# One chained run for the output matmuls of a half unit, in place of two pieces

## The chip, the cores and the metric

The kernel runs on one core of a Trainium2 chip. The metric is the device time of one execution in microseconds (us). TensorE is PE in the profile (PEld is its weight load), VectorE is DVE, ScalarE is ACT, GpSimd is POOL, and SyncE, which issues most DMAs, is SP.

## The reference

Two stages follow each other: a complex, element-wise decaying recurrence over time, and a feed-forward product.

```python
# q, k, v, a_re, a_im: (4, 8, 768, 48), f32
for t in range(S):
    new_re = ar * S_re - ai * S_im          # ar, ai: a_re, a_im scaled to a magnitude below 1
    new_im = ar * S_im + ai * S_re
    S_re, S_im = new_re + k_t (x) v_t, new_im
    y[:, :, t] = einsum('bhd,bhde->bhe', q[:, :, t], S_re)
x = y as (3072, 384)
out = ((x @ w_a) * (x @ w_b)) @ w_out       # w_a, w_b: (384, 1536), w_out: (1536, 384)
```

## The kernel before, in words

The recurrence is cut into 12 units: two pairs of batches, six chunks of 128 time steps each. A unit `u` holds two batches, its halves `i = 0, 1`; each half has 8 heads and 128 time steps. `prep(u)` computes, almost wholly on DVE with some ACT, the running products of the decays and multiplies q and k by them. Twelve DMAs (`stack`, L346) bring the result from the tile `qk` into `stk`, where each head lies by itself.

`attn(u)` is then the attention of the unit as matmuls. For each half and each group `hg` of four heads:

- `scores` (L379): k times q of four heads into a PSUM tile `pm`; DVE multiplies it by the causal mask into `am` (L382).
- `transposes` (L390): the keys, through PSUM, into `kt`.
- `outputs` (L419): for all heads of the half, `v_t` times `am` and, from the second chunk on, the state `u` times `stk`, into the PSUM tile `xp`. Each of these matmuls fills only 32 columns of the array; the four column groups (`qd`) are issued one after the other. ACT casts `xp` to `xh` (L423), and `residual` gives the rest `xl` (L429 on DVE, or L431 and L434).
- `state` (L444): the keys times v, which DVE adds to the state `u` (L451, L455).

The feed-forward of unit `w` runs in a loop over 12 blocks `f`: `gemm1` (L488) makes two products in a PSUM tile `ab`, ACT and DVE make `h_t`, `hh` and `hl` from it (L496 to L499), and `gemm2` (L506) sums into `o`, two blocks later. While the feed-forward of unit `w` runs, the pieces of `attn(w + 1)` are handed out between its blocks (`slot`), and `prep(w + 3)` goes along in the same way. The first unit's preparation and the splitting of the weights (L134 to L149, with matmuls L147 and L148) come first.

The order in which the instructions stand on each engine is not the order of the code: a scheduler in the language's tile layer sorts them by priority and by its own estimate of when the inputs are there. `tc.high_priority` moves what it holds ahead. On the chip each engine then works through its list in that order, and an instruction that waits holds those behind it. The list built from the kernel before is, matmul by matmul, the list that the profile shows.

In f32 a matmul of the scores, outputs or states shows as two instructions in the profile and as one in the listings of order: 32 output matmuls of a half (16 in the first chunk, where there is no state) are 64 (32) rows of L419.

Of the kernel before, what the change touches and what calls it, by code (L numbers as in the profile page):

```python
# [8 lines left out]
F32 = mybir.dt.float32  # L9
# [10 lines left out]
C = 128  # L20
NCH = S // C
NBP = B // 2
NU = NBP * NCH
NJ = 3
# [29 lines left out]
ATTN_FIRST = 2000  # L54
# [4 lines left out]
def view(ap, offset, dims):  # L59
    return bass.AP(tensor=ap.tensor, offset=ap.offset + offset, ap=[list(ap.ap[0])] + dims)  # L60
# [7 lines left out]
def tile_kernel(ctx: ExitStack, tc: tile.TileContext, a_d, qk_d, v_d, w_d, qn_d, kn_d, vn_d, an_d, out_d):  # L68
    nc = tc.nc
    vec, act, pe, sync = nc.vector, nc.scalar, nc.tensor, nc.sync  # L70
# [12 lines left out]
    ps_x = fast.enter_context(tc.tile_pool(name="ps_x", bufs=1, space=PSUM))  # L83
# [35 lines left out]
    def r(ap):  # L119
        return ap.bitcast(F32R)  # L120
# [76 lines left out]
    def rescaled(c):  # L197
        return c % 2 == 1 and c + 1 < NCH
# [160 lines left out]
    quads = [[] for _ in range(4)]  # L359
# [5 lines left out]
    def attn(u, xh, xl):  # L365

        c = u % NCH
        last = c + 1 == NCH
        ams, kts, xps = {}, {}, {}

        def cols(i):
            return slice(i * C, (i + 1) * C), slice(TOK + i * C, TOK + (i + 1) * C)

        def scores(i, hg):
            qs, ks = cols(i)
            sp = ps_m.tile([128, 4, 128], F32, name="pm")
            for h4 in range(4):
                h = hg * 4 + h4
                pe.matmul(out=sp[:, h4], lhsT=stk[:, h, ks], rhs=stk[:, h, qs], start=True, stop=True)  # L379
            am = kvp.tile([128, 512], F32, name="am", bufs=2).rearrange("p (h t) -> p h t", h=4)  # L380
            with tc.high_priority(offset=ATTN_FIRST):
                vec.tensor_tensor(out=am, in0=sp, in1=mask[:].unsqueeze(1).broadcast_to([128, 4, 128]),  # L382
                                  op=ALU.mult)
            ams[i, hg] = am

        def transposes(i, hg):
            qs, ks = cols(i)
            tp = ps_m.tile([128, 512], F32, name="pm")
            for h4 in range(4):
                pe.transpose(out=tp[:, h4 * KS:(h4 + 1) * KS], in_=stk[0:KS, hg * 4 + h4, ks],  # L390
                             identity=ident[0:KS, 0:KS])
            kt = kvp.tile([128, 4, KS], F32, name="kt", bufs=2)
            with tc.high_priority(offset=ATTN_FIRST):
                act.copy(out=kt.rearrange("p h k -> p (h k)"), in_=tp[:, 0:4 * KS])
            kts[i, hg] = kt

        def outputs(i, half):
            qs, ks = cols(i)
            v_t = v_tiles[u, i]
            if half == 0:  # L400
                xps[i] = ps_x.tile([128, NJ, C], F32, name="xp")
            xp = xps[i]
            work = []
            for qd in range(4):
                lst = []
                for ti, pieces in quads[qd]:
                    mm = []
                    for h, off in pieces:
                        mm.append((v_t[:, off:off + 32], ams[i, h // 4][:, h % 4, :]))
                        if c > 0:  # L410
                            mm.append((us[i][:, off:off + 32], stk[:, h, qs]))
                    for n, (l, rr) in enumerate(mm):
                        lst.append((ti, l, rr, not lst, n == len(mm) - 1))
                work.append(lst)
            ns = len(work[0])
            for n in range(half * ns // 2, (half + 1) * ns // 2):
                for qd in range(4):
                    ti, l, rr, st, sp_ = work[qd][n]
                    pe.matmul(out=xp[qd * 32:(qd + 1) * 32, ti], lhsT=l, rhs=rr, start=st, stop=sp_,  # L419
                              tile_position=(0, qd * 32), skip_group_check=True)  # L420
            if half == 1:
                with tc.high_priority(offset=ATTN_FIRST):
                    act.copy(out=r(xh[:, :, qs]), in_=xp)  # L423

        def residual(i, _):
            qs, ks = cols(i)
            if u > 1:
                with tc.high_priority(offset=ATTN_FIRST):
                    vec.tensor_tensor(out=r(xl[:, :, qs]), in0=xps[i], in1=xh[:, :, qs], op=ALU.subtract)  # L429
                return  # L430
            pe.matmul(out=xps[i], lhsT=r(nident), rhs=r(xh[:, :, qs]), start=False, stop=True,  # L431
                      skip_group_check=True)
            with tc.high_priority(offset=ATTN_FIRST):
                act.copy(out=r(xl[:, :, qs]), in_=xps[i])  # L434

        def state(i, hg):
            ut, v_t = us[i], v_tiles[u, i]
            own = u >= OWN_FROM
            n = D if own else 2 * D
            kp = ps_m.tile([128, 512], F32, name="pm")  # L440
            for h4 in range(4):
                h = hg * 4 + h4
                o = (h // 2) * 128 + (h % 2) * (80 if own else 32)
                pe.matmul(out=kp[0:KS, h4 * n:(h4 + 1) * n], lhsT=kts[i, hg][:, h4, :],  # L444
                          rhs=v_t[:, o:o + n], start=True, stop=True)
            uv = view(ut[0:KS], hg * 256, [[128, 2], [80, 2], [1, 48]])
            kv = view(kp[0:KS], 0, [[2 * n, 2], [D if own else 3 * D, 2], [1, D]])
            sv = view(stk[0:KS], hg * 4 * RUN + 2 * TOK + i, [[2 * RUN, 2], [RUN, 2], [0, 48]])
            with tc.high_priority(offset=ATTN_FIRST):
                if c > 0:  # L450
                    vec.tensor_tensor(out=uv, in0=kv, in1=uv, op=ALU.add)  # L451
                else:
                    act.copy(out=uv, in_=kv)
                if rescaled(c):
                    vec.tensor_tensor(out=uv, in0=uv, in1=sv, op=ALU.mult)  # L455

        order = [(scores, 0, 0), (scores, 0, 1), (transposes, 0, 0), (transposes, 0, 1),
                 (outputs, 0, 0), (outputs, 0, 1), (scores, 1, 0), (residual, 0, 0), (state, 0, 0), (scores, 1, 1),
                 (state, 0, 1), (transposes, 1, 0), (transposes, 1, 1), (outputs, 1, 0),
                 (outputs, 1, 1), (state, 1, 0), (residual, 1, 0), (state, 1, 1)]  # L460
        if u == 0:
            order = [(scores, 0, 0), (scores, 0, 1), (outputs, 0, 0), (outputs, 0, 1), (scores, 1, 0), (scores, 1, 1),
                     (residual, 0, 0), (outputs, 1, 0), (outputs, 1, 1), (transposes, 0, 0), (transposes, 0, 1),
                     (residual, 1, 0), (state, 0, 0), (state, 0, 1), (transposes, 1, 0), (transposes, 1, 1),
                     (state, 1, 0), (state, 1, 1)]
        for fn, i, g in order:
            if not (last and fn in (transposes, state)):
                fn(i, g)
                yield

    def pieces(u):
        return 12 if u % NCH + 1 == NCH else 18

    def new_x():
        return (moe.tile([128, NJ, TOK], F32, name="xh"), moe.tile([128, NJ, TOK], F32, name="xl"))
# [158 lines left out]
    for _ in attn(0, *x_cur):  # L634
        drain(p1, P1_A)
# [13 lines left out]
    for w in range(NU):  # L649
        last = w + 1 == NU  # L650
        x_nxt = None if last else new_x()
        at = None if last else attn(w + 1, *x_nxt)
        if not last:
            load_v(w + 1)
# [112 lines left out]
```

## Time and profile before

| | us |
|---|---|
| median of three runs (697.93 to 698.81) | 698.0 |
| span of the profiled execution, first to last instruction | 696.3 |
| median less span: what lies around the instructions | 1.7 |
| PE busy | 654.4 (94%) |
| DVE busy | 550.4 (79%) |
| ACT busy | 311.4 (45%) |

The profile's chain is the sequence of work that ended last, each step followed back to what released it. The granted TensorE clock is 0.970 over the span and full from about 60 us on. Matmuls are pipelined, so the length of a row of PE is not what it costs; what counts is the time from the start of one row to the start of the next, and the chain gives just that for merged rows.

### The profile page before, as it was taken

Reading aid. Unit: us, or ns where it says so; the run is one execution under the profiler, and the core shown is the slowest. Engines: PE = TensorE matmul, PEld = TensorE weight load, DVE = VectorE, ACT = ScalarE, POOL = GpSimd, SP = SyncE. Lnnn points to the kernel's source line nnn. Section 1 sums busy time; section 2 is a strip of 40 time slices with the busy share of each in tenths; the row PEclk is TensorE's granted clock in tenths of the full one; section 3 lists DMA queues with packets and bytes.
Section 4 is the critical chain, followed back from the end, with each engine's and each line's share of the span. In section 5 each row is a group of like instructions: output and inputs, shape, how many; then the busy total and the mean of one; then the engine's idle time right before and its main releaser. Section 6 shows DMA issues by size and latency. Waiting matters only on the chain.

```text
span 696.3 us, 14288 instructions
## 1 busy us (share of the span) xinstructions
PE 654.4 (94%) x5842; PEld 610.3 (88%) x5842; DVE 550.4 (79%) x1259; ACT 311.4 (45%) x622; POOL 5.6 (1%) x11
## 2 busy tenths in 40 slices
PE   3658999999999999999999999999999999999996
PEld 1224789899999999999999999999999999999996
DVE  6999899998878889989899898999989863233221
ACT  6347665635545346255363554535542332221221
POOL 3000000000000000000000000000000000000000
PEclk9566999999999999999999999999999999999999
DMA  8963301413314215134051340611500500400000
GB/s 314 403 263 92 121 1 44 141 54 88 111 39 137 63 39 152 46 108 128 17 162 44 109 127 2 171 64 48 162 29 5 164 24 17 106 24 2 24 1 28
DMA packets 30232, 63.94 MB, mean 92 GB/s; under 512 B 3664, under 2 KB 7248, under 8 KB 30160
## 3 DMA queue, kind: packets, MB, share of 16 engines
q1 hardware_dynamic: 26704, 58.23, 26.9%
q10 hardware_dynamic: 3456, 4.72, 1.9%
q8 instruction: 48, 0.79, 0.5%
q14 instruction: 24, 0.20, 0.1%
HBM read 39.32 MB, written 4.72 MB: 63 GB/s over the span
## 4 chain that ended last, share of the span: by engine, by line
PE 62%; DVE 27%; DMA 4%; ACT 3%; issue 2%; SPq 1%; ACTq 0%; DVEq 0%
PE ab L488 29%; PE o L506 15%; PE xp L419 6%; PE pm L379 5%; PE pm L444 4%; DVE a_t L289 3%; DVE qk L309 3%; DMA w<-in_dram 2%; DVE hl L499 2%; DVE pr L227 2%; DVE h_t L497 2%; PE pm L390 2%; DVE z L294 2%; DMA stk<-qk 2%; PE pm L147 2%
## 5 line engine op out<-in xcount | busy, mean ns | idle before, releaser
L488 PE MATMUL ab<-xh,w 128*128 128x256 f32 x1728 | 340.1, 285 | 0.0
L488 PEld LDWEIGHTS ab<-xh,w 128*128 128x128 f32 x1728 | 277.0, 189 | 2.0 <-issue 1.4
L488 PE MATMUL ab<-xl,w 128*128 128x256 f32 x864 | 245.1, 284 | 0.0
L488 PEld LDWEIGHTS ab<-xl,w 128*128 128x128 f32 x864 | 162.9, 189 | 0.6 <-issue 0.2
L506 PE MATMUL o<-w,hh 128*128 128x384 f32 x576 | 153.0, 345 | 0.0
L496 ACT COPY h_t<-ab 128x256 f32<-128x256 f32 x144 | 53.3, 370 | 185.5 <-PE ab L488 184.8
L497 DVE TENSOR_TENSOR h_t<-ab,h_t 128x256 f32<-128x256 f32 x144 | 60.5, 420 | 72.4 <-ACT h_t L496 72.0
L506 PEld LDWEIGHTS o<-w,hh 128*128 128x128 f32 x576 | 96.9, 188 | 3.3 <-issue 2.8
L506 PE MATMUL o<-w,hl 128*128 128x384 f32 x288 | 97.7, 340 | 0.0
L498 ACT CAST hh<-h_t 128x256 fp32r<-128x256 f32 x144 | 58.0, 403 | 74.5 <-DVE h_t L497 73.9
L499 DVE TENSOR_TENSOR hl<-h_t,hh 128x256 fp32r<-128x256 f32 x144 | 60.4, 420 | 14.2 <-ACT hh L498 14.1
L379 PE MATMUL pm<-stk 128*128 128x128 f32 x384 | 55.2, 280 | 2.6 <-DMA stk<-qk 2.6
L147 PE MATMUL ab<-o_sb,ident 128*128 128x384 f32 x42 | 29.6, 806 | 28.9 <-DVE o_sb L138 28.9
L379 PEld LDWEIGHTS pm<-stk 128*128 128x128 f32 x384 | 49.4, 192 | 6.9 <-issue 5.5
L506 PEld LDWEIGHTS o<-w,hl 128*128 128x128 f32 x288 | 54.1, 188 | 0.4 <-issue 0.4
L227 DVE TENSOR_TENSOR pr<-z 128x384 f32<-128x384 f32 (+1 forms) x91 | 47.2, 525 | 4.0 <-ACT z L213 2.1
L289 DVE TENSOR_TENSOR a_t<-z,b_t 128x768 f32<-128x768 f32 x48 | 44.9, 952 | 0.0
L147 PEld LDWEIGHTS ab<-o_sb,ident 128*128 128x128 f32 x42 | 10.2, 286 | 39.5 <-DVE o_sb L138 29.4
L419 PE MATMUL xp<-am,v_t 128*32 128x128 f32 x768 | 42.5, 277 | 2.2 <-DVE am L382 1.9
L309 DVE TENSOR_TENSOR qk<-qk,z 128x1536 f32<-128x1536 f32 (+1 forms) x26 | 42.3, 1625 | 0.0
L382 DVE TENSOR_TENSOR am<-pm,mask 128x512 f32<-128x512 f32 x48 | 32.8, 686 | 5.7 <-PE pm L379 5.6
L419 PE MATMUL xp<-stk,u 128*32 128x128 f32 x640 | 34.2, 273 | 0.0
(107 smaller groups left out, 758.3 us busy)
## 6 DMA issues: line engine op xcount, KB each, us to landing
w<-in_dram SPq DMA_DIRECT2D x36, 384.0 KB, 8.0
qk<-in_dram SPq DMA_DIRECT2D x12, 768.0 KB, 4.8
stk<-qk SPq DMA_DIRECT2D x48, 192.0 KB, 3.4
a_t<-in_dram SPq DMA_DIRECT2D x11, 768.0 KB, 4.3
v_t<-in_dram SPq DMA_DIRECT2D x24, 256.0 KB, 2.7
stk<-qk SPq DMA_DIRECT2D x24, 192.8 KB, 3.3
out_dram<-o_sb ACTq DMA_DIRECT2D x24, 192.0 KB, 1.9
stk<-qk SPq DMA_DIRECT2D x16, 128.0 KB, 3.2
```

Of the source, the lines that this page charges most:

```text
L147: pe.matmul(out=lp[:, 0:n], lhsT=ident, rhs=t, start=True, stop=False)
L227: vec.tensor_tensor(out=pr[:, :, :, o:o + n], in0=view(zz, W + at_(i) + 2 * o, [[W, 2], [-W, 2], [2, n]]), in1=tok(slice(1, 3), i - 1, o, ...
L289: vec.tensor_tensor(out=pz[:, s].rearrange("p (j b e) -> p j b e", j=SUB // 2, e=2), in0=zb[:, 1 + s], in1=view(bb, (1 + k - s) * NB, [[0, ...
L309: vec.tensor_tensor(out=qk4[:, :, k, x0:x1], in0=qk4[:, :, 1, x0:x1], in1=z[:, k].rearrange("p (j t) -> p j t", j=NJ).unsqueeze(2).broadca ...
L379: pe.matmul(out=sp[:, h4], lhsT=stk[:, h, ks], rhs=stk[:, h, qs], start=True, stop=True)
L419: pe.matmul(out=xp[qd * 32:(qd + 1) * 32, ti], lhsT=l, rhs=rr, start=st, stop=sp_, tile_position=(0, qd * 32), skip_group_check=True)
L488: pe.matmul(out=ab[:, m * TOK:(m + 1) * TOK], lhsT=r(w_ab(f, part, m * NJ + i)), rhs=r(xt[:, i, :]), start=n == 0, stop=n == 8)
L496: act.copy(out=h_t, in_=ab[:, 0:TOK])
L497: vec.tensor_tensor(out=h_t, in0=ab[:, TOK:2 * TOK], in1=h_t, op=ALU.mult)
L498: act.copy(out=r(hh), in_=h_t)
L499: vec.tensor_tensor(out=r(hl), in0=h_t, in1=hh, op=ALU.subtract)
L506: pe.matmul(out=os_[tt][:, 0:DM], lhsT=r(ht[:, ts]), rhs=r(w_t[f, 2][:, part, :]), start=(f == 0 and n == 0), stop=(f == NF - 1 and n == 2))
```

## The change

The two calls of `outputs` per half (`half` 0 and 1) become one. All output matmuls of the half stand in one call with high priority, and each is tied behind the one before it (`tc.issue_after`), so that the scheduler keeps them in one row. The order within the run is turned round: the last head groups and the last column group come first. The count of pieces for `slot` goes from 18 to 16 (12 to 8 in a unit without states). The matmuls themselves, their operands and their number are the same.

```diff
-        def outputs(i, half):
+        def outputs(i, _):
...
-            if half == 0:
-                xps[i] = ps_x.tile([128, NJ, C], F32, name="xp")
+            xps[i] = ps_x.tile([128, NJ, C], F32, name="xp")
...
-                for ti, pieces in quads[qd]:
+                for ti, pieces in reversed(quads[qd]):
...
-            ns = len(work[0])
-            for n in range(half * ns // 2, (half + 1) * ns // 2):
-                for qd in range(4):
-                    ti, l, rr, st, sp_ = work[qd][n]
-                    pe.matmul(out=xp[qd * 32:(qd + 1) * 32, ti], lhsT=l, rhs=rr, start=st, stop=sp_,
-                              tile_position=(0, qd * 32), skip_group_check=True)
-            if half == 1:
-                with tc.high_priority(offset=ATTN_FIRST):
-                    act.copy(out=r(xh[:, :, qs]), in_=xp)
+            run = None
+            with tc.high_priority(offset=ATTN_FIRST):
+                for n in range(len(work[0])):
+                    for qd in (3, 2, 1, 0):
+                        ti, l, rr, st, sp_ = work[qd][n]
+                        with ExitStack() as behind:
+                            if run is not None:
+                                behind.enter_context(tc.issue_after(run))
+                            run = pe.matmul(out=xp[qd * 32:(qd + 1) * 32, ti], lhsT=l, rhs=rr, start=st, stop=sp_,
+                                            tile_position=(0, qd * 32), skip_group_check=True).ins
+                act.copy(out=r(xh[:, :, qs]), in_=xp)
...
     def pieces(u):
-        return 12 if u % NCH + 1 == NCH else 18
+        return 8 if u % NCH + 1 == NCH else 16
```

In the lists `order` of `attn`, the pair `(outputs, i, 0), (outputs, i, 1)` becomes `(outputs, i, 0)`.

What it does to PE's list is seen at three places. Behind the change the line numbers from L419 on are higher: the output matmul is L422, `gemm1` L489, `gemm2` L507, the states L445.

First, PE in unit 3, first half, before. The output matmuls (`xp`) begin, and other work comes between them.

```order
L390 MATMUL pm<-ident,stk 128x96 x4
L419 MATMUL xp<-am,v_t 32x128 x4
L419 MATMUL xp<-stk,u_111 32x128 x4
L419 MATMUL xp<-am,v_t 32x128
L379 MATMUL pm<-stk 128x128
L419 MATMUL xp<-am,v_t 32x128 x2
L488 MATMUL ab<-xh,w_947 128x256
L506 MATMUL o_1588<-w_836,hh 128x384
...
L488 MATMUL ab<-xl,w_999 128x256
L419 MATMUL xp<-am,v_t 32x128
L419 MATMUL xp<-stk,u_111 32x128 x4
```

The same place in the changed kernel.

```order
L489 MATMUL ab<-xh,w_999 128x256
L379 MATMUL pm<-stk 128x128
L422 MATMUL xp<-am,v_t 32x128 x4
L422 MATMUL xp<-stk,u_111 32x128 x4
L422 MATMUL xp<-am,v_t 32x128 x4
L422 MATMUL xp<-stk,u_111 32x128 x4
L422 MATMUL xp<-am,v_t 32x128 x4
L422 MATMUL xp<-stk,u_111 32x128 x4
L422 MATMUL xp<-am,v_t 32x128 x4
L422 MATMUL xp<-stk,u_111 32x128 x4
L379 MATMUL pm<-stk 128x128 x3
```

Three pieces of 9, 2 and 21 matmuls, two of them ending inside a group of four column groups, have become one run of 32, which stands behind the scores of all heads of the half.

Second, PE in unit 7, second half, before.

```order
L390 MATMUL pm<-ident,stk 128x96 x4
L419 MATMUL xp<-am,v_t 32x128 x4
L419 MATMUL xp<-stk,u_112 32x128 x4
L419 MATMUL xp<-am,v_t 32x128 x4
L419 MATMUL xp<-stk,u_112 32x128 x4
L506 MATMUL o_4818<-w_836,hh 128x384 x2
L506 MATMUL o_4818<-w_836,hl 128x384
L506 MATMUL o_4819<-w_836,hh 128x384 x2
L506 MATMUL o_4819<-w_836,hl 128x384
L419 MATMUL xp<-am,v_t 32x128 x4
```

And in the changed kernel.

```order
L507 MATMUL o_4818<-w_767,hl 128x384
L507 MATMUL o_4819<-w_767,hh 128x384
L422 MATMUL xp<-am,v_t 32x128 x4
L422 MATMUL xp<-stk,u_112 32x128 x4
...
L422 MATMUL xp<-am,v_t 32x128 x4
L422 MATMUL xp<-stk,u_112 32x128 x4
L507 MATMUL o_4819<-w_767,hh 128x384
L507 MATMUL o_4819<-w_767,hl 128x384
L390 MATMUL pm<-ident,stk 128x96 x8
```

Two pieces of 16 with a block of `gemm2` between them have become one run, and it stands earlier, ahead of the transposes.

Third, PE in unit 5, second half, from the scores of its second head group on, before.

```order
L379 MATMUL pm<-stk 128x128 x4
L506 MATMUL o_3586<-w_775,hh 128x384 x2
L506 MATMUL o_3586<-w_775,hl 128x384
L506 MATMUL o_3587<-w_775,hh 128x384 x2
L506 MATMUL o_3587<-w_775,hl 128x384
L419 MATMUL xp<-am,v_t 32x128 x4
L419 MATMUL xp<-stk,u_112 32x128 x4
L419 MATMUL xp<-am,v_t 32x128 x3
L488 MATMUL ab<-xh,w_937 128x256
L419 MATMUL xp<-am,v_t 32x128
```

And in the changed kernel.

```order
L379 MATMUL pm<-stk 128x128 x4
L489 MATMUL ab<-xh,w_937 128x256
L489 MATMUL ab<-xl,w_937 128x256
L489 MATMUL ab<-xh,w_937 128x256 x2
L489 MATMUL ab<-xl,w_937 128x256
L489 MATMUL ab<-xh,w_937 128x256 x2
L489 MATMUL ab<-xl,w_937 128x256
L489 MATMUL ab<-xh,w_937 128x256
L489 MATMUL ab<-xh,w_947 128x256
L422 MATMUL xp<-am,v_t 32x128 x4
```

Between these scores and the first output matmul stand 10 matmuls of `gemm1`, where 6 of `gemm2` stood, and the first output matmul now reads the second head group's `am`, which before was first read by the eighth matmul with `am`, the last row shown.

Over the whole list the output matmuls stood in 46 separate runs and now stand in 24, one for each half. Of the 22 breaks that are gone, 13 ended inside a group of four column groups (two in unit 0, four in unit 1, four in unit 2, two in unit 3, one in unit 5) and 9 at the end of a group (one each in units 3, 4, 5 and 6 to 11). DVE, ACT and SP keep their instructions and their counts; on DVE the rows of one unit move by some places against each other.

More of the change, by code (lines that the diff above doesn't have):

```diff
@@ L457, in attn @@
         order = [(scores, 0, 0), (scores, 0, 1), (transposes, 0, 0), (transposes, 0, 1),
-                 (outputs, 0, 0), (outputs, 0, 1), (scores, 1, 0), (residual, 0, 0), (state, 0, 0), (scores, 1, 1),
+                 (outputs, 0, 0), (scores, 1, 0), (residual, 0, 0), (state, 0, 0), (scores, 1, 1),
                  (state, 0, 1), (transposes, 1, 0), (transposes, 1, 1), (outputs, 1, 0),
-                 (outputs, 1, 1), (state, 1, 0), (residual, 1, 0), (state, 1, 1)]
+                 (state, 1, 0), (residual, 1, 0), (state, 1, 1)]
         if u == 0:
-            order = [(scores, 0, 0), (scores, 0, 1), (outputs, 0, 0), (outputs, 0, 1), (scores, 1, 0), (scores, 1, 1),
-                     (residual, 0, 0), (outputs, 1, 0), (outputs, 1, 1), (transposes, 0, 0), (transposes, 0, 1),
+            order = [(scores, 0, 0), (scores, 0, 1), (outputs, 0, 0), (scores, 1, 0), (scores, 1, 1),
+                     (residual, 0, 0), (outputs, 1, 0), (transposes, 0, 0), (transposes, 0, 1),
                      (residual, 1, 0), (state, 0, 0), (state, 0, 1), (transposes, 1, 0), (transposes, 1, 1),
```

## The prediction

> **What bounds the kernel now.** I read the page's busy times first, then the time by stages, then the chain of waits in order of time. Busy shares and two stretches (columns: busy us and instructions of PE, PEld, DVE, ACT, POOL, then clock, DMA share, GB/s):
>
> ```profile
> PE 654.4 (94%) x5842; PEld 610.3 (88%) x5842; DVE 550.4 (79%) x1259; ACT 311.4 (45%) x622; POOL 5.6 (1%) x11
> ...
> 77.00:145.00 68.00, 67.97 (x566) 60.36 (x565) 65.52 (x152) 44.05 (x90) 0.00 (x0) 1.00 0.21 63
> ...
> 302.00:349.00 47.00, 46.51 (x446) 44.88 (x446) 42.98 (x91) 21.31 (x41) 0.00 (x0) 1.00 0.29 88
> ```
>
> PE is busy all the time, but an average hides who is waited for: from 77 to 145 us DVE is busy for 65.52 of 68 us as well. The chain tells the stages apart (start, length, what; "stk<-qk" is the DMA that hands `prep`'s result to the scores):
>
> ```profile
> 169.41 3.40 DMA stk<-qk
> ...
> 172.95 0.46 PE pm L379 x2
> ...
> 213.83 1.67 DVE qk L309
> ...
> 217.53 3.37 DMA stk<-qk
> ...
> 269.27 4.11 DMA stk<-qk
> ...
> 273.52 0.46 PE pm L379 x2
> ...
> PE pm L379 <- DMA stk<-qk: 2.6, 3, 1.6
> ```
>
> Three times the scores wait for DVE's last products and a DMA, in units 2, 3 and 4; the last row, of the view of waits, puts PE's idle time there at 2.6 us. Behind 273.5 us the chain does not leave PE for a DMA again. So time saved on PE counts in full from 273.5 us on; ahead of that it counts only as far as DVE gets its products done earlier, and the rest becomes a longer wait at the three places.
>
> **The change part by part.** First the price of a break in the output run, in starts to starts, from the chain. Unit 3's first half has three pieces, with 18, 4 and 42 of 64 rows; unit 10's first half has one, its second half two clean ones:
>
> ```profile
> 224.59 0.22 PE pm L379 x2
> ...
> 226.15 0.77 PE xp L419 x18
> 226.92 0.42 PE pm L379 x2
> 227.34 0.34 PE xp L419 x4
> ...
> 230.15 0.44 PE pm L379 x2
> 230.59 1.43 PE xp L419 x42
> ...
> 579.59 1.89 PE xp L419 x64
> 581.47 1.24 PE o L506 x6
> ...
> 583.60 2.16 PE ab L488 x18
> ...
> 587.36 1.06 PE o L506 x6
> ...
> 591.91 1.01 PE xp L419 x32
> 592.92 1.26 PE o L506 x6
> 594.18 1.01 PE xp L419 x32
> ```
>
> Whole, the run takes 1.89 us. In three pieces it takes 0.77 + 0.34 + 1.43 = 2.54, and the two pairs of scores ahead of a re-entry take 0.42 and 0.44 where an undisturbed pair takes 0.22. That is 0.65 + 0.42 = 1.07 us for two breaks, 0.53 each: breaks that leave a group of four column groups part-filled. In two clean pieces it takes 2.02, and the block of `gemm2` between them 1.26 against 1.06: 0.13 + 0.20 = 0.33 for a clean break; I take 0.3, since in the changed list some runs cut into a `gemm1` or `gemm2` block. With 13 part-filled and 9 clean breaks gone, PE's list is shorter by 13 x 0.53 + 9 x 0.3 = 9.6 us.
>
> The Trainium skill bears on this price: "TensorEngine Tiling (Array Packing)", section Key Properties, says that a change of the tiling mode drains the engine, while a change of the tile within a mode does not. By that alone every break would cost the same, 22 x 0.33 = 7.3 us; the rows above make a part-filled one dearer.
>
> Of the 9.6 us, by place:
>
> - Units 4 to 11, behind 273.5 us: one part-filled and eight clean breaks, 0.53 + 8 x 0.3 = 2.9 us, all on the path.
> - Units 2 and 3: six part-filled and one clean, 3.5 us, ahead of the waits at 221 and 273 us. It counts only as DVE's idle time for PE shrinks (for PE itself, or by way of ACT), which is, from 172 to 221 us (first four rows) and from 221 to 274 us (last two; columns: total us, times, longest):
>
> ```profile
> DVE am L382 <- PE pm L379: 1.4, 3, 0.8
> ...
> DVE xl L429 <- ACT xh L423: 0.7, 1, 0.7
> DVE h_t L497 <- ACT h_t L496: 0.5, 2, 0.3
> ...
> DVE u L451 <- PE pm L444: 0.4, 1, 0.4
> ...
> DVE h_t L497 <- ACT h_t L496: 2.0, 4, 0.9
> DVE am L382 <- PE pm L379: 1.6, 2, 1.0
> ```
>
>   That is 3.0 us in unit 2 and 3.6 in unit 3, so 3.5 us would fit, but a saving behind a wait does nothing for that wait. Ends 0.5 and 3.5; I take the middle, 2.0.
> - Units 0 and 1: six part-filled breaks, 3.2 us, while DVE is 96% busy (65.52 of 68). From 130 to 172 us its waits for PE are
>
> ```profile
> DVE am L382 <- PE pm L379: 0.8, 1, 0.8
> ...
> DVE u L451 <- PE pm L444: 0.3, 1, 0.3
> ```
>
>   so no more than 1.1 us can come through; I take 0.6, ends 0 and 1.1.
>
> What the change adds is a wait. Before, a run could start on the first head group's `am`. Now its first matmul needs the second group's `am`, and that stands little PE work ahead: in unit 5's second half 10 matmuls of `gemm1`, each 2.16 / 18 = 0.12 us by the row of 18 above, 1.2 us. Rows of the timeline (a row's length here is till its last matmul ends):
>
> ```profile
> 334.55 1.05 PE L379 MATMUL pm<-stk 128*128 128x128 f32 x8
> ...
> 338.24 0.30 PE L419 MATMUL xp<-am,v_t 128*32 128x128 f32 x1 [0.49 <-DVE am L382]
> ...
> 429.48 1.05 PE L379 MATMUL pm<-stk 128*128 128x128 f32 x8
> ...
> 430.57 0.69 DVE L382 TENSOR_TENSOR am<-pm,mask 128x512 f32<-128x512 f32 x1 [0.42 <-PE pm L379]
> ...
> 337.47 0.72 DVE L382 TENSOR_TENSOR am<-pm,mask 128x512 f32<-128x512 f32 x1
> ...
> 435.26 0.68 DVE L382 TENSOR_TENSOR am<-pm,mask 128x512 f32<-128x512 f32 x1
> ```
>
> With DVE idle, `am` is there 0.73 us behind the end of the scores (430.53 to 431.26): covered by the 1.2 us of work. With DVE in the middle of `prep`, it is there 2.59 us behind (335.60 to 338.19): PE would wait 1.4. The wait at 338.24 is of this kind already, and goes with the break (0.5 us more gained). In units 4 to 11 `am` of the second group was later than the new lead in seven halves of sixteen, by 0.2 to 1.5 us, 3.2 us together. But in units 7 to 9 PE waited for the same `am` before, at the transposes, which need the PSUM tile that it frees:
>
> ```profile
> PEld pm L390 <- DVE am L382: 1.8, 5, 0.5
> ```
>
> So part of the new wait takes the place of an old one. Ends 0 and 3.2, I take 1.5. Behind a waiting run stand `gemm1` and `gemm2`; ACT and DVE then get `ab` later, but three buffers of `ab` stand between.
>
> The rest costs nothing: the number of instructions and DMAs is the same; `xh` and `xl` are read only by the next unit's `gemm1`, 5 us and more behind the runs; and the fewer pieces for `slot` move scores and transposes by less than a block.
>
> The sum: -2.9 - 0.5 - 2.0 - 0.6 + 1.5 = -4.5 us. The profiled execution's span is 696.3 us, 1.7 below the median of 698.0, and I take what lies around it as unchanged: span 691.8, time 693.5 us (0.6% faster). A difference below 0.2% (1.4 us) can't be told from none here.
>
> **The rivals.**
>
> *The product of the mask takes the break's place (not faster, or slower).* Every one of the 20 runs of units 2 to 11 now starts on the second `am`. What speaks for it: DVE is 91% busy from 302 to 349 us (42.98 of 47), and an `am` behind one 1.67 us `qk` product or two `a_t` products is later than the lead. Against: DVE was idle for the scores at 430.57, and mostly is within one short instruction. The gain of 6.0 us is used up at a mean wait of 0.3 us for each run; at a mean of 0.5 us it is 698.0 - 6.0 + 10 = 702 us, slower. The Trainium skill ("TensorE: Matmul & The Clock Gate", Part 2, Step-by-step) says that TensorE pulls weight loads ahead but keeps matmuls in program order; by that rule all of the feed-forward behind a waiting run stands still, and the wait of 0.49 us at 338.24, with `gemm1` ready behind it, agrees.
>
> *The early saving is all lost, and the wait is at its upper end (no change).* DVE sets the three landings of `stk`; then -2.9 - 0.5 + 3.2 = -0.2, about 697.8 us. For it speaks that DVE's list keeps its length; against it the DVE waits for PE in units 2 and 3.
>
> *All of PE's shorter list arrives.* 698.0 - 9.6 - 0.5 = 687.9 us with no new wait. For it: PE is 94% busy. Against it: the 96% of DVE up to 145 us.
>
> That the change does not do what it says is no case here: the built list has 24 runs.
>
> **How the numbers follow.** The forecast 0.68, the `am` wait as the bound 0.10, the early saving lost 0.14, everything arrives 0.08. Faster than by 0.2%: 0.68 + 0.08 = 0.76; within 0.2%: 0.14; slower: 0.10. The forecast's own range, with the ends of its terms: -2.9 - 0.5 - 3.5 - 1.1 + 0 = -8.0 and -2.9 - 0.5 - 0.5 - 0 + 3.2 = -0.7, 690.0 to 697.3 us. The second rival is taken in up to 698.2; the first and the third stay outside.
>
> **What would show it.** Right: 24 runs of L422 of 1.9 us (1.0 in the first chunk), `gemm2` blocks of 1.06 us between them no longer at 1.26; PE's waits for DMA stk<-qk longer than the 2.6 us of now by some 2 to 4 us, with their places earlier than 221 and 273 us by 1 to 2 us; new rows "PE xp <- DVE am" of one to three us in total; the stretch behind the last of them shorter by about 2 us. Wrong: if "xp <- DVE am" is over 6 us, if the scores of units 2 to 4 start no earlier than now, or if a run of 64 rows takes clearly more than 1.9 us in its new order of column groups.

## The result, and the profile after

| | before | changed |
|---|---|---|
| median, us | 698.0 (697.93 to 698.81) | 690.64 (690.11 to 691.38, four runs) |
| span of the profiled execution, us | 696.3 | 688.5 |

The ratio is 0.9898, 95% interval 0.9882 to 0.9915: 7.4 us or 1.05% faster. The forecast was 693.5 us, 4.5 us faster, with a range from 690.0 to 697.3 us: the result lies 0.6 us inside its fast end. Of the twelve executions of the kernel with the cut at 18, further down, two were slow ones (919 and 1066 us), and its time is the median of the other ten.

From the view of the chain of the changed kernel: unit 3's first half (225.93) and unit 10's second half (581.40) with what stands around them (start, length, what).

```profile
223.92 0.50 PE ab L489 x4
224.42 0.22 PE pm L379 x2
224.64 0.08 PE pm L390
224.72 1.21 PE ab L489 x10
225.93 1.88 PE xp L422 x64
...
580.80 0.59 PE o L507 x3
581.40 1.89 PE xp L422 x64
583.28 0.73 PE o L507 x3
```

Each half is one run of 64 rows, 1.88 or 1.89 us long: the new order of the column groups costs nothing, and the pieces of 18, 4 and 42 rows and of 32 and 32 are gone. The second run cuts into a block of `gemm2`, which takes 0.59 + 0.73 = 1.32 us where an undisturbed one takes 1.06; that is the one way in and out that every run still has.

PE's waits over the whole span (total us, times, longest):

```profile
PE xp L422 <- DVE am L382: 4.1, 5, 2.2
PE pm L379 <- DMA stk<-qk: 2.0, 2, 1.4
```

Those behind unit 4's first scores, from 268 us on:

```profile
PE xp L422 <- DVE am L382: 1.6, 3, 0.8
PE pm L390 <- DVE am L382: 0.5, 1, 0.5
```

And before, from 273 us on:

```profile
PE xp L419 <- DVE am L382: 0.5, 1, 0.5
PE pm L390 <- DVE am L382: 0.3, 1, 0.3
```

The new wait for the second head group's product is there. The longest, 2.2 us, stands in unit 0; here is its row of the timeline:

```profile
69.79 1.93 PE L422 MATMUL xp<-am,v_t 128*32 128x128 f32 x32 [2.22 <-DVE am L382]
```

In units 4 to 11 the waits at the run are 1.6 us in total, where 0.5 stood before; with the wait at the transposes PE waits there 2.1 us for DVE's mask product instead of 0.8. The wait for `stk` is not longer than before but shorter, 2.0 against 2.6 us.

All later readings use three stretches of the trace, cut at the first row of the scores of units 0, 2 and 4, and the stretch ahead of them. The numbers of breaks are counted from the built list.

| kernel | to unit 0's scores | to unit 2's | to unit 4's | to the end | span |
|---|---|---|---|---|---|
| before | 62.5 | 110.4 | 99.4 | 424.0 | 696.3 |
| changed | 61.2 | 109.9 | 96.5 | 420.8 | 688.5 |
| difference | -1.3 | -0.5 | -2.8 | -3.1 | -7.8 |

### The profile page after: what moved, and what is told of

Its sections match the earlier page's. It is cut to its first block, busy times and chain, and to the rows that moved or that the text cites. A ratio compares the mean times of both kernels' runs of the same rounds, so it can differ in the third digit from the quotient of the medians.

```text
span 688.5 us, 14290 instructions
## 1 busy us (share of the span) xinstructions
PE 644.5 (94%) x5842; PEld 608.3 (88%) x5842; DVE 550.1 (80%) x1259; ACT 310.1 (45%) x622; POOL 5.6 (1%) x11
## 4 chain that ended last, share of the span: by engine, by line
PE 66%; DVE 25%; ACT 4%; DMA 2%; issue 2%; SPq 0%; DVEq 0%; ACTq 0%
PE ab L489 33%; PE o L507 16%; PE xp L422 5%; PE pm L379 4%; PE pm L445 3%; DVE a_t L289 3%; DVE qk L309 2%; PE pm L390 2%; DVE h_t L498 2%; DVE hl L500 2%; PE pm L147 1%; DVE z L294 1%; DVE pr L227 1%; DVE am L382 1%; DVE pb L262 1%
## 5 line engine op out<-in xcount | busy, mean ns | idle before, releaser
L489 PE MATMUL ab<-xh,w 128*128 128x256 f32 x1728 | 341.6, 286 | 0.0
L489 PEld LDWEIGHTS ab<-xh,w 128*128 128x128 f32 x1728 | 277.2, 189 | 1.7 <-issue 0.8
L489 PE MATMUL ab<-xl,w 128*128 128x256 f32 x864 | 245.5, 284 | 0.0
L489 PEld LDWEIGHTS ab<-xl,w 128*128 128x128 f32 x864 | 163.0, 189 | 0.6 <-issue 0.2
L507 PE MATMUL o<-w,hh 128*128 128x384 f32 x576 | 152.7, 343 | 0.0
L507 PEld LDWEIGHTS o<-w,hh 128*128 128x128 f32 x576 | 96.6, 188 | 1.1 <-issue 1.0
L507 PE MATMUL o<-w,hl 128*128 128x384 f32 x288 | 97.2, 338 | 0.0
L147 PE MATMUL ab<-o_sb,ident 128*128 128x384 f32 x42 | 28.1, 764 | 29.7 <-DVE o_sb L138 29.7
L507 PEld LDWEIGHTS o<-w,hl 128*128 128x128 f32 x288 | 54.1, 188 | 0.0
L422 PE MATMUL xp<-am,v_t 128*32 128x128 f32 x768 | 37.7, 281 | 4.3 <-DVE am L382 4.1
L424 ACT CAST xh<-xp 128x384 fp32r<-128x384 f32 x24 | 11.4, 475 | 49.3 <-PE xp L422 49.1
```

The lines of the kernel that those rows point to most:

```text
L147: pe.matmul(out=lp[:, 0:n], lhsT=ident, rhs=t, start=True, stop=False)
L422: run = pe.matmul(out=xp[qd * 32:(qd + 1) * 32, ti], lhsT=l, rhs=rr, start=st, stop=sp_, tile_position=(0, qd * 32), skip_group_check=True ...
L489: pe.matmul(out=ab[:, m * TOK:(m + 1) * TOK], lhsT=r(w_ab(f, part, m * NJ + i)), rhs=r(xt[:, i, :]), start=n == 0, stop=n == 8)
L507: pe.matmul(out=os_[tt][:, 0:DM], lhsT=r(ht[:, ts]), rhs=r(w_t[f, 2][:, part, :]), start=(f == 0 and n == 0), stop=(f == NF - 1 and n == 2))
```

## The experiments

Every median stands against that of the kernel before from the same chip, 698.0 to 698.3 us. The stretches are those of the table above.

**Only the order turned round.** The kernel before with its two pieces, without priority and without the tie.

```diff
-                for ti, pieces in quads[qd]:
+                for ti, pieces in reversed(quads[qd]):
...
-                for qd in range(4):
+                for qd in (3, 2, 1, 0):
                     ti, l, rr, st, sp_ = work[qd][n]
```

> The kernel before (two pieces for each half, no priority for the matmuls, no chain) with only the order inside turned round: last head groups and last column group first. Its built list has 33 output runs: the 13 part-filled breaks are gone, 9 clean ones are left (one each in units 3, 4, 5 and 6 to 11). Theory (the time goes with the breaks): 13 x 0.53 us of PE's list is gone as in the change, and 9 x 0.3 = 2.7 us is left, so about 2.4 us above the changed kernel's 690.6: 693.0 us (692 to 694). Rival A (one call with priority is what matters, since the run stands earlier): close to the kernel before, 696 to 698 us. Rival B (the waits for the second head group's mask product cost as much as the clean breaks): as the changed kernel, 690.0 to 691.2 us.

Measured: 694.06 us, ratio 0.994 (0.9926 to 0.9953), at the upper end of what was expected; stretches 61.8, 109.9, 96.6 and 423.6 us. The turned order alone gives 4.1 of the 7.4 us, all of the early part among it. A likely reason, which no run tests by itself, is that the first output matmul now waits for the later mask product, so that the scheduler begins a run only when it can finish it. One clean break is left in each of units 3 to 11. The chain of this kernel in unit 10, second half:

```profile
587.70 1.01 PE xp L419 x32
588.71 1.25 PE o L506 x6
589.97 1.01 PE xp L419 x32
```

By these rows the break costs (2.02 - 1.89) + (1.25 - 1.06) = 0.32 us. Behind unit 4 there are eight, and that stretch is 423.6 - 420.8 = 2.8 us longer than in the changed kernel, 0.35 us for each. The two kernels differ in the counts of pieces as well, to which a run below comes back.

**One call, priority and tie without the turned order.**

```diff
-                for ti, pieces in reversed(quads[qd]):
+                for ti, pieces in quads[qd]:
...
-                    for qd in (3, 2, 1, 0):
+                    for qd in range(4):
```

> The changed kernel with the order inside the run turned back: first head groups and first column group first; one call, priority and chain stay. The scheduler then puts other work into the run again: 46 runs, 22 of them cut at 11 of 32 (7 of 16), inside a group of four. Theory (breaks): 22 part-filled breaks x 0.53 = 11.7 us of PE's list come back against 9.6 in the kernel before, so 698 to 700 us, with the part behind unit 4's first score slower than in the kernel before by 7 x 0.53 + 0.3 less 8 clean ones x 0.3. Rival (the chain and the single call are what matters): 690 to 692 us.

Measured: 701.1 us, ratio 1.0044 (1.003 to 1.0058), slower than before. The chain of this kernel in unit 10, first half:

```profile
575.66 0.79 PE xp L422 x22
576.45 0.37 PE o L507
576.82 1.43 PE xp L422 x42
```

22 and 42 rows take 0.79 + 1.43 = 2.22 us for 1.89, and the single matmul between them 0.37 instead of 1.06 / 6 = 0.18: 0.52 us for this part-filled break, as the prediction priced it. Behind unit 4 there are 14 of them, and the stretch takes 429.3 us, 8.5 more than in the changed kernel: 0.6 each, the waits at the cut among it. The tie keeps the order of the run but lets other work in. Taking the tie alone out of the changed kernel gives the same list of instructions on every engine; that kernel was not run. So of "one chained run" the chain is the part that does nothing here.

**The single run in units 4 to 11 only, and in units 0 to 3 only.** Both kernels hold the two forms of `outputs` side by side and choose by the unit; the counts of pieces go with the form.

```diff
+        if not (u >= 4):        # the other kernel: u < 4
+            order = [(outputs_two, i, g) if fn is outputs else (fn, i, g) for fn, i, g0 in order
+                     for g in ((0, 1) if fn is outputs else (g0,))]
```

> The single run in units 4 to 11 only; units 0 to 3 as before with two pieces. 37 runs: 9 breaks gone (one part-filled, eight clean). Theory (behind unit 4 PE alone sets the time): the 3.1 us that the changed kernel gained from unit 4's first score on, 694.9 us (694.3 to 695.6). Rival (the late part's gain needs the earlier start of DVE and is lost to the waits on the mask product): 696.5 to 698 us.

Measured: 694.47 us, ratio 0.9949 (0.9936 to 0.9963). This is what was expected of a late part that counts by itself. The last stretch is 420.6 us, as in the changed kernel; the third is 99.4, as before.

> The single run in units 0 to 3 only; units 4 to 11 as before with two pieces. 32 runs: 12 part-filled breaks and two clean ones less. Theory: what came through ahead of unit 4's first score in the changed kernel's trace, 4.7 us, of which 1.4 us stands ahead of any output matmul and may be chance: 693.3 to 694.7 us. Rival (DVE sets the early part, nothing comes through): 696.5 to 698 us.

Measured: 692.79 us, ratio 0.9922 (0.9908 to 0.9935), 0.5 us faster than the expectation's end. The third stretch is 96.6 us, as in the changed kernel. The last is 423.1, 0.9 below before, though units 4 to 11 have the old form: in this kernel's list the scheduler no longer makes unit 5's part-filled break. Apart from that the two halves of the change are separate, and each stretch takes the value of its own form.

**The single run in units 2 and 3, in unit 2, and in units 0 and 1.** The same kernel with `u in (2, 3)`, `u == 2` and `u < 2`.

> The single run in units 2 and 3 only, the rest as before. 39 runs: six part-filled breaks and one clean one less, 3.5 us of PE's list. The prediction let 2.0 us of it through. Theory now (unit 2's runs stand on PE's part of the chain that ends at DVE's h_t, and DVE waits there only for PE): nearly all, 3.0 to 3.5 us, 694.7 to 695.2 us. Rival (the early gain of the change is in units 0 and 1 and the start): 0 to 1 us, 697.2 to 698.2 us.

Measured: 694.54 us, ratio 0.9952 (0.9938 to 0.9966), 0.2 us faster than the expectation's end. The third stretch is 96.1 us, 3.3 below before, of 3.5 us that PE's list is shorter. The early saving is not halved.

> The single run in unit 2 only. Four part-filled breaks less there, 2.1 us of PE's list, and the scheduler takes the part-filled one of unit 5 too (0.5 us and its wait). Theory (unit 2's runs stand on PE's part of the chain up to DVE's h_t at 213 us, so the whole saving comes through): scores of unit 3 start about 2 us earlier against those of unit 2, 2.0 to 2.8 us in all: 695.4 to 696.2 us. Rival (half of it comes through, as the prediction took it): 1.0 to 1.5 us, 696.7 to 697.2 us.

Measured: 695.06 us, ratio 0.9962 (0.9948 to 0.9975), 2.9 us, a little beyond the range. The third stretch is 97.6 us: 1.8 of the 2.1 us come through; another 0.7 us is gained behind unit 4, where unit 5's part-filled break is gone. DVE's waits from unit 2's to unit 3's scores in the changed kernel, against the first four rows of the prediction's fence:

```profile
DVE h_t L498 <- ACT h_t L497: 1.3, 3, 0.6
...
DVE am L382 <- PE pm L379: 0.3, 1, 0.3
```

Before, DVE waited 1.4 us there for the scores, 0.7 for `xh` and 0.4 for the states. What is left is 0.3 for the scores, and the others are gone; `h_t` went from 0.5 to 1.3 us. So 2.2 us of DVE's waits went and 0.8 came. Two other waits for ACT, at `a_t` (L303) and `hl`, are shorter by 0.3 us each, so that DVE waits 2.0 us less in all, and the time from unit 2's to unit 3's scores is 46.0 us instead of 48.1. In the chain of the changed kernel the hand-over to unit 3 starts here:

```profile
213.63 3.37 DMA stk<-qk
```

That is 3.9 us earlier than the 217.53 us of before; 1.3 us of it is the earlier start, which a second profile of the changed kernel, further down, shows to be chance, and the rest comes with the runs.

> The single run in units 0 and 1 only. Six part-filled breaks less there; the scheduler then gives unit 3's first half one break more (5, 4, 2, 21) and takes the part-filled one of unit 5. Theory (DVE sets the time up to the first wait for stk, and waits for PE only 1.1 us there): 0.5 to 1.1 us faster than the kernel before, 697.1 to 697.7 us. Rival (PE's shorter list counts there too): 3.2 us, 695 us.

Measured: 697.09 us, ratio 0.9986 (0.9977 to 0.9995), 0.9 us. The second stretch is 109.9 us, 0.5 below before; the third is 0.5 us longer, where the scheduler gave unit 3 a further break; the last is 423.2, 0.7 below before, with unit 5's part-filled break gone. So the median lies in the range expected, but most of its gain is unit 5's, and only the second stretch speaks for units 0 and 1.

**A break put back by force, at the end of a group and in its middle.** In units 4, 5, 7, 8, 9 and 10 the first head group's transposes are tied into the run, behind its 16th or its 18th matmul, and stand nowhere else; these units have 14 pieces in place of 16. The two built lists differ in the place of the cut alone. In the second halves of units 4, 7, 8, 9 and 10 other work stands in the cut too, ahead of the transposes, since the tie does not keep it out.

```diff
+                        given += 1
+                        if given == 16 and u in CUT:      # the other kernel: 18
+                            run = transposes(i, 0, run)
```

> The changed kernel with a clean break put back by force: in units 4, 5, 7, 8, 9 and 10, in both halves, the four transposes of the first head group are tied into the chain behind the 16th output matmul, and stand nowhere else. 36 runs: 12 clean breaks more than the changed kernel. Theory (price by break): 12 x 0.3 = 3.6 us above the changed kernel's 690.6: 694.2 us (693.2 to 695). Rival (the breaks cost nothing, the gain came from where the runs stand): 690.6 us, since the runs start at the same places.

Measured: 695.67 us, ratio 0.9966 (0.9954 to 0.9978), 1.5 us above the expectation and 0.7 beyond its range. The last stretch is 425.1 us, 4.3 above the changed kernel's for 12 clean breaks: 0.36 each.

> As e_cut16, with the same four transposes behind the 18th output matmul instead, which is the middle of a group of four column groups: 12 part-filled breaks, all else alike. Theory (a part-filled break costs 0.53 against 0.3 to 0.33): 12 x 0.2 to 0.23 = 2.4 to 2.8 us above e_cut16, 696.6 to 697 us. Rival (only the change of the tiling mode costs, as the Trainium skill's page TensorEngine Tiling (Array Packing), Key Properties, would have it): the same as e_cut16.

Measured: 697.6 us, ratio 0.9996 (0.9985 to 1.0007), 1.9 us above the kernel with the cut at 16; by the last stretch, 427.1 us, 2.0 above it. That is a little less than the 2.4 us expected, and far from the rival's nothing. The chain of the kernel with the cut at 16, in unit 7's first half:

```profile
422.34 1.08 PE xp L428 x32
423.42 0.48 PE pm L394 x4
423.90 1.01 PE xp L428 x32
```

And of the kernel with the cut at 18:

```profile
420.76 1.29 PE xp L428 x36
422.05 0.48 PE pm L394 x4
422.53 1.00 PE xp L428 x28
```

The transposes between cost the same, 0.48 us; the run's two parts take 1.29 + 1.00 = 2.29 instead of 1.08 + 1.01 = 2.09 us. The 32 matmuls of the half make 8 groups of four when cut at 16, and 9 when cut at 18, two of them half filled: the additional group costs 0.20 us by these rows and 2.0 / 12 = 0.17 by the stretch, most of the 0.24 that a full group takes (64 rows in 1.89 us, eight rows to a group). One price for every break, as the prediction works it out from the Trainium skill's page "TensorEngine Tiling (Array Packing)", Key Properties, which says that a change of the tiling mode drains the engine, falls short by that step.

**The run without priority.** The copy to `xh` keeps it; the list still has 24 runs.

```diff
-            with tc.high_priority(offset=ATTN_FIRST):
+            with ExitStack():
                 for n in range(len(work[0])):
...
-                act.copy(out=r(xh[:, :, qs]), in_=xp)
+                with tc.high_priority(offset=ATTN_FIRST):
+                    act.copy(out=r(xh[:, :, qs]), in_=xp)
```

> The changed kernel without the high priority for the output matmuls; chain, turned order and single call stay. Still 24 runs, but from unit 3's second half on they stand 1.5 to 7 us of PE work behind their last scores where the changed kernel has 1.0 to 2.7. Theory (what is left to gain are the waits for the second head group's mask product behind unit 4, 1.6 us in the view of waits): these go, but the transposes then wait for the same PSUM tiles as they did before, so 0 to 1.6 us faster than the changed kernel: 689.0 to 690.6 us. Rival (the early start of the run is itself worth time, since xh, xl and the state follow from it): 691.5 us or more.

Measured: 691.11 us, ratio 0.9896 (0.988 to 0.9912), no different from the changed kernel and 0.5 us above the expectation. From 268 us on, PEld's waits for the mask product in the changed kernel:

```profile
PEld xp L422 <- DVE am L382: 3.5, 8, 1.0
...
PEld pm L390 <- DVE am L382: 1.0, 2, 0.7
```

And in this kernel, where no row of `xp` is left among them:

```profile
PEld pm L390 <- DVE am L382: 2.6, 6, 0.8
```

With later runs the wait at the run is gone, and the transposes wait for the PSUM tile that the same product frees. The wait belongs to DVE's product, not to the run. PE itself waits 1.0 us for that product behind unit 4 instead of 2.1, and yet the last stretch, 421.1 us, is no shorter: the view of waits does not tell what the waits cost.

**The counts of pieces, and a second look.**

```diff
-        return 8 if u % NCH + 1 == NCH else 16
+        return 12 if u % NCH + 1 == NCH else 18
```

> The changed kernel with the counts of pieces for the slots put back to 18 and 12. Still 24 runs; rows of the states and the scores move by less than a block. Theory: nothing, 690.0 to 691.4 us. Rival (the spread of the pieces over the slots is part of the gain): 692 us or more.

Measured: 691.78 us, ratio 0.9912 (0.9899 to 0.9926): 0.4 us beyond the expectation, and the interval overlaps that of the changed kernel. The last stretch is 421.9 us, 1.0 longer than the changed kernel's. The counts may be worth up to 1 us; it is not settled. Against this kernel, which has its counts, the one with only the order turned takes 423.62 - 421.86 = 1.76 us longer behind unit 4, 0.22 for each of the eight clean breaks and not 0.35. So that kernel puts the clean break between 0.22 and 0.35 us; its rows say 0.32.

> The changed kernel once more, for a second profile. In the first one everything up to unit 0's first scores, ahead of any output matmul, was 1.35 us earlier than in the kernel before. Theory (chance, from the start of the loads and the splitting of the weights): another start, 61.0 to 63.7 us, and the stretch from there on within 0.5 us of the first profile. Rival (the change moved something ahead of them): 61.2 us again.

Measured: 691.23 us, ratio 0.9906 (0.9888 to 0.9924). Unit 0's scores stand at 62.7 us, 1.5 later than in the first profile, and the other stretches are 110.1, 96.5 and 420.7 us, within 0.2. So the 1.3 us ahead of the first scores are chance and no part of the change. Over all profiles here that start lies between 61.2 and 63.7 us.

No kernel of these beats the changed one.

## Why the prediction was right, and where sizes were off

By the three stretches the change is worth 6.5 us in the first profile and 6.4 in the second, against the one profile of before; the medians differ by 7.4 us, and the rest is of the size by which the start varies.

- **The price of a break.** Right. Part-filled: forecast 0.53; 0.52 by the rows of the kernel with the order turned back, 0.53 by the forced cut at 18 (6.3 us / 12). Clean: forecast 0.3, taken below the 0.33 of its rows; 0.36 by twelve forced ones, 0.32 by the rows of the kernel with only the order turned, and 0.22 to 0.35 by its last stretch. That the two kinds differ was right too: the cuts at 16 and 18 lie 2.0 us apart.
- **Units 4 to 11, "all on the path".** The single run there alone gives the whole of the last stretch's 3.1 us, so this part does not depend on the early one. But the reason, that the chain does not leave PE for a DMA, looked at the DMA alone: behind 273.5 us the chain lies on DVE for some 113 of 418 us before, and for 90 of 416 behind 268 us in the changed kernel, in four long pieces that end at a mask product. The second of them ends so in the changed kernel:

```profile
417.21 0.61 DVE am L382
417.82 0.04 issue
417.87 0.55 PE pm L390 x4
```

  A part of PE's shorter list therefore comes back as waits, 1.3 us by the view of waits (2.1 for 0.8).
- **The sum for that stretch, -2.9 - 0.5 + 1.5 = -1.9.** Too little by 1.2 us, and the runs do not settle which term had the wrong size. The new wait at the run was forecast as 1.5 us and shows as 1.6. With breaks of 0.35 and 0.53 and unit 5's old wait, 8 x 0.35 + 0.53 + 0.5 = 3.8 us are saved; then all that the change adds costs 0.7 us, half of what was taken, and the kernel without priority speaks for waits that cost less than they show. Or the waits cost what they show, and the counts of pieces, which the prediction put at nothing, give the missing 1 us, as the run with the old counts would have it.
- **Units 2 and 3, "I take the middle, 2.0".** Too low: 2.7 to 3.3 us in the eight profiles with the single run in both units, near the upper end of 3.5. This step failed by its reason, "a saving behind a wait does nothing for that wait": no row stood behind it, and DVE's waits for PE in the prediction's own fence, 3.0 and 3.6 us, were large enough for all of the saving.
- **Units 0 and 1, 0.6 us.** The second stretch is 110.4 to 111.1 us in the four kernels with the old form there (the one before, and the single run in units 4 to 11, in 2 and 3, and in 2 alone) and 109.6 to 110.1 in the nine others with the turned order; the means, 110.9 and 109.9, differ by 1.0 us. Right within its ends, 0 and 1.1. That DVE is the bound fits: the kernel with the order turned back keeps four of the six part-filled breaks there and still has 109.5 us, so taking away more breaks gave nothing more.
- **"PE's waits for DMA stk<-qk longer by some 2 to 4 us".** Wrong: 2.0 us instead of 2.6. DVE's products came forward with PE, so no longer wait was left. For the same reason the scores of units 3 and 4 came forward by more than the 1 to 2 us expected: by 2.5 and 3.3 us from unit 0's scores on.
- **The rivals.** The mask product as the bound: PE's waits for it at the run were 1.6 us in total over the 16 halves of units 4 to 11, 0.1 each, a third of the 0.3 at which it would have used up the gain. The early saving lost: no. All of it arrives, 687.9 us: nearer than reckoned, 2.7 us below the result; what is missing is mostly units 0 and 1, where 2.2 of 3.2 us do not arrive.
- **What the prediction did not see.** Which edit does it. It read the change as a chain; the runs show that the turned order does most and the tie nothing, and that the single call, with priority or without it, takes away the nine clean breaks that the turned order leaves.

What stays open: the price of the new waits apart from that of the breaks behind unit 4, since the kernels compared there differ in their waits and their counts too, and the worth of the pieces' counts.

## What to carry to other kernels

Matmuls that use a part of the array's columns are cheap only together: price each break in their run from starts to starts, in the rows on both sides of it, and count a part-filled group as a whole step. Where a scheduler sorts by when inputs are ready, try putting first the instruction whose input comes last: here it alone took 13 of the 22 breaks away. A tie that only keeps the order does not hold other work out. And when time is saved on an engine that hands work to another, add up that other engine's waits for it stage by stage: where they are larger than the saving, as in units 2 and 3 here, nearly all of it can come through.

## What the runs showed of the hardware

Leaving a run of 32-column matmuls for full-width ones and coming back cost 0.32 to 0.36 us by the rows and the forced cuts, about as much as three `gemm1` matmuls of 0.12. A group of four column tiles that is left part-filled takes most of the time of a full one, 0.17 to 0.20 us of 0.24. In two executions of the same kernel the start up to the first scores differed by 1.5 us, while each of the later stretches repeated within 0.2 us.
